# Strided sparse attention feeding a squared-ReLU MLP on one Trainium2 core: moving DMA transposes two groups later and one pair of steps past each other

## The chip, the core and the metric

The kernel runs on one core of a Trainium2 chip. A core has five engines with their own instruction streams: TensorE (PE; its weight loads are listed as PEld), VectorE (DVE), ScalarE (ACT), GpSimd (POOL) and SyncE (SP). SP only issues DMA transfers here; POOL issues some too. The metric is the device time of one execution in microseconds (us). Before the change the median of four runs is 313.06 us.

## What is computed

Inputs are q, k, v of shape (8, 8, 576, 64) and two weights, w_in (512 x 2048) and w_out (2048 x 512), in fp32.

```
scores = q k^T / 8
heads 0-3: keep  0 <= row - col < 32              (local)
heads 4-7: keep  row >= col and row = col mod 32  (strided)
attn   = softmax(scores) v            for every batch and head
x      = attn, heads side by side     4608 x 512
out    = relu(x w_in)^2 w_out         4608 x 512
```

## The kernel before, in words

**Units.** The attention is cut into 32 units, u = 4 b + p: batch b, pair of heads p. Pairs 0 and 1 are local, 2 and 3 strided. A local head has six blocks of 96 rows; a strided head has eight groups of 72 rows (rows are brought together by their number mod 8, and a mask picks the right ones).

**Steps of a unit.** They are small closures in a list:

- `step_T(u, "q")`, `step_T(u, "k")`: PE transposes q or k into PSUM (L271), ACT or DVE copies the result to SBUF (L284, L286). Only early units have them (`has_T`: local units of batches 0 to 3, strided ones of batches 0 and 1). For later ones DMA transposes do this work: `transpose_str` (L161, both strided pairs of a batch at once, from a bf16 copy in DRAM that POOL's casting DMA has written, L153) and `transpose_local` (L173).
- `step_S(u)`: scores on PE (L315) into four PSUM banks, the exponential on ACT (L320), and, on DVE, the mask (L326).
- `step_D(u, part)`: the PV step. PE multiplies the exponentials with v and a column of ones (L419), DVE takes the reciprocal of the sums (L433) and multiplies (L434) into `x_l` (local) or `x_s` (strided). Local units have two parts, strided ones three.
- `step_E(u)`: brings the result, transposed, into `xt[p]`, the left operand of the MLP. Local units of batches 2 to 7 do it with one DMA transpose on SP's queue (L444). Others use PE transposes (L451) and a copy (L457 to L459).
- `step_X(u)`: for strided units of batches 6 and 7, a store to DRAM and a DMA transpose back (L471, L473), the second of them six groups later.

**The MLP.** It runs in 9 chunks of 512 rows. `mm1(c, ff)` is a group of four matmuls of 512 columns (L487) over the four pairs in the order 0, 1, 2, 3, and then a ReLU on ACT (L493) and a square on DVE (L494). `mm2(c, i)` is a group of four matmuls with w_out (L527); each fourth one ends a block of 128 rows, which ACT copies to `y` (L531) and SP stores (L532). Rows of batch b are 576 b to 576 b + 575, so chunk 2 needs batches 1 and 2, chunk 3 batches 2 and 3, chunk 4 batches 3 and 4, chunk 5 batches 4 and 5.

**What sets the order.** Everything is written out by hand at build time. Units of batch 0 go first (`first_steps`). Then a list of groups (mm1 and mm2) is walked through; ahead of each group come as many attention steps as a due table says, and the hooks of that place (loads of later batches). The list of steps is made by `stream_steps`, once for batch 1 and once for the rest. `later(n, fn)` puts something off by n groups: `tick`, after each group, runs what is due.

Each engine works through its own stream in order, and a waiting instruction holds up all behind it. For the change the following matter:

- On PE, in batch 1: S(5), T(6, q), D(4, 0), T(6, k), D(4, 1), S(6), with groups of mm2 between them. D(4, 0) needs v of unit 4, which POOL's casting DMA loads (L214) and whose last 32 rows of each block POOL then shifts (L221). The same POOL stream has issued, ahead of that, the four transfers of v for the strided units 6 and 7 (L227).
- PSUM tiles of the attention come from a pool of five banks that go round in the order of the program (`ps_t`).
- On SP: loads of q, k, v (L107, L113, L185, L201), the DMA transposes and the stores of y, all in one queue. Each of the eight semaphores that tell of landings is used in turn, so a transfer isn't issued before the one eight places ahead of it has landed.

Of the kernel before, what the change touches and what calls it, by code (L numbers as in the profile page):

```python
# [14 lines left out]
def kernel(  # L15
# [9 lines left out]
    nc = tc.nc  # L25
# [69 lines left out]
    def is_local(u):  # L95
        return units[u][1] < H // 4
# [146 lines left out]
    def later(n, fn, key=None):  # L243
        pending.append((clock[0] + n, key, fn))
# [12 lines left out]
    def step_T(u, name):  # L257
        s = st[u]
        local = is_local(u)
        n, w = (6, QL) if local else (NJ, SP_)  # L260
        src = s[name]
        if u != 1:
            src = src.rearrange("p j h d -> p (j h d)" if local else "p h c -> p (h c)")
        pt = ps_t.tile([128, S], BF16, name="pt")
        for j in range(n):
            if u == 1:
                for h in range(2):
                    nc.tensor.transpose(pt[64 * h:64 * h + 64, w * j:w * (j + 1)],
                                        src[:, h, D * j:D * (j + 1)], ident[0:w, 0:w])
            else:  # L270
                nc.tensor.transpose(pt[:, w * j:w * (j + 1)], src[:, 128 * j:128 * (j + 1)],  # L271
                                    ident[0:w, 0:w])
        if local and name == "k":
            full = kTl[v_slot(u)]
            dst = full[:, 32:32 + S]
        else:
            full = dst = qkT.tile([128, S], BF16, name=f"{name}T")
        if local:
            o = dst.rearrange("c (p j) -> c p j", j=6)
            i = pt.rearrange("c (j p) -> c p j", j=6)  # L280
        else:
            o, i = dst, pt
        if name == "q" and u not in (1, 2, 3):
            nc.scalar.copy(o, i)  # L284
        else:
            nc.vector.tensor_copy(o, i)  # L286
        s[name + "T"] = full
# [149 lines left out]
    def step_E(u):  # L437
        s = st[u]
        b, p = units[u]
        x = s["x"]  # L440
        local = is_local(u)
        n, w = (NL, QL) if local else (NJ, SP_)
        if local and b >= XB:
            nc.sync.dma_start_transpose(  # L444
                out=xt[p][:, b * S:(b + 1) * S].rearrange("c (t q) -> c t q", q=QL),
                in_=x.rearrange("p n d -> p (n d)"))
            st.pop(u)
            return
        px = ps_t.tile([128, S], BF16, name="pt")
        for t in range(n):  # L450
            nc.tensor.transpose(px[:, w * t:w * (t + 1)],  # L451
                                x[:, 2 * t:2 * t + 2, :].rearrange("p h d -> p (h d)"),
                                ident[0:w, 0:w])
        dst = xt[p][:, b * S:(b + 1) * S]
        copy = nc.scalar.copy if u < 12 else nc.vector.tensor_copy
        if local:
            copy(dst, px)  # L457
        else:
            copy(dst.rearrange("c (p j) -> c p j", j=NJ),  # L459
                                  px.rearrange("c (j p) -> c p j", j=NJ))  # L460
        st.pop(u)
# [3 lines left out]
    def by_dram(u):  # L465
        return not is_local(u) and units[u][0] >= XD

    def step_X(u):
        b, p = units[u]
        t = dram.tile([S, 2 * D], BF16, name="x_d")  # L470
        nc.sync.dma_start(out=t.rearrange("(p j) c -> p (j c)", j=NJ),  # L471
                          in_=st.pop(u)["x"].rearrange("p n d -> p (n d)"))
        later(6, lambda: nc.sync.dma_start_transpose(out=xt[p][:, b * S:(b + 1) * S], in_=t))  # L473
# [60 lines left out]
    T_ = lambda u, nm: (lambda: step_T(u, nm))  # L534
    S_ = lambda u: (lambda: step_S(u))
    D_ = lambda u, part: (lambda: step_D(u, part))
    E_ = lambda u: (lambda: step_E(u))

    idle_w = y_pool.tile([128, 512], FP32, name="y").bitcast(BF16)
# [49 lines left out]
    def has_T(u):  # L589
        return units[u][0] < (LB if is_local(u) else XB)  # L590

    def stream_steps(lo, hi, order, ends, last=None):
        add_ = order.append

        def finish(u):
            if not by_dram(u):
                add_(E_(u))
                ends[u] = len(order)

        if last is None:  # L600
            add_(T_(lo, "q"))
        else:
            finish(last)
        for i in (T_(lo, "k"), T_(lo + 1, "q"), S_(lo), T_(lo + 1, "k"), lambda: None):
            add_(i)
        for u in range(lo, hi):
            if u + 1 < hi:
                add_(S_(u + 1))
            if u + 2 < hi and has_T(u + 2):
                add_(T_(u + 2, "q"))  # L610
            if u > lo and is_local(u):
                finish(u - 1)
            add_(D_(u, 0))
            if u > lo and not is_local(u):
                finish(u - 1)
            if u + 2 < hi and has_T(u + 2):
                add_(T_(u + 2, "k"))
            add_(D_(u, 1))
            if not is_local(u):
                add_(D_(u, 2))  # L620
            if by_dram(u):
                add_(lambda u=u: step_X(u))
                ends[u] = len(order)
        if hi < 4 * B:
            add_(T_(hi, "q"))
        else:
            finish(hi - 1)
# [96 lines left out]
    NCH = T // 512  # L724
    steps, ends = [], {}
    stream_steps(4, 8, steps, ends)
    stream_steps(8, 4 * B, steps, ends, last=7)
    groups = []
    starts = {}
# [113 lines left out]
```

## Time and profile before

| | us |
|---|---|
| median of 4 runs | 313.06 |
| the runs | 312.82, 313.30, 314.43, 311.17 |
| the profiled execution, its own time | 312.82 |
| its span, first to last instruction | 310.9 |
| PE busy | 300.0 (96%) |
| PE weight loads | 148.4 (48%) |
| DVE busy | 166.7 (54%) |
| ACT busy | 162.8 (52%) |
| POOL busy | 90.1 (29%) |
| SP's DMA queue | 72528 packets, 32.98 MB |
| POOL's DMA queue | 19552 packets, 10.98 MB |

All durations below come from the one profiled execution; 1.9 us of its time lie outside of its span. A row of a timeline gives the start, the length, the engine (SPq is SP's queue), the line of the code, the operation, its output and inputs, shapes, a count where instructions were merged, and in brackets idle time of the engine ahead of it with what ended it. Matmuls overlap, so lengths of neighbouring rows on PE add up to more than the time between them. For a transfer the row shows its issue; when it landed is told by the completion records of the trace.

### The profile page before, as it was taken

How to read it: one execution, taken by the hardware profiler on the slowest of the kernel's cores; microseconds unless marked ns; L12 is line 12 of the kernel's file. 1: busy time of each engine (PE TensorE's matmuls, PEld its weight loads, DVE VectorE, ACT ScalarE, POOL GpSimd, SP SyncE). 2: the span in 40 equal slices, each digit the busy share in tenths (PEclk: the TensorE clock that was granted, in tenths of full speed). 3: DMA queues.
4: the chain of work that ended last, by engine and by line, in shares of the span. 5: the costliest groups of instructions: out<-in, count | busy, mean ns of one | idle time of the engine just before them, and what ended most of it. 6: DMA issues, size and time to landing. Idle time of an engine off the chain costs nothing.

```text
span 310.9 us, 6192 instructions
## 1 busy us (share of the span) xinstructions
PE 300.0 (96%) x2368; PEld 148.4 (48%) x2368; DVE 166.7 (54%) x411; ACT 162.8 (52%) x338; POOL 90.1 (29%) x117
## 2 busy tenths in 40 slices
PE   7889897999999999999999999999999999999995
PEld 3534454544555544454444454444444444444444
DVE  7675666379766886576467676654422222222200
ACT  3957654387654765555555555655443434344311
POOL 8528864554720723381066033000000000000000
PEclk9999999799999999999999999999999999999999
DMA  7999999999999999999999792224122010000021
GB/s 143 155 206 215 210 191 259 215 260 195 198 136 230 206 211 162 201 246 209 158 225 205 167 207 78 73 72 55 53 76 84 34 37 34 34 34 36 39 96 67
DMA packets 92252, 44.40 MB, mean 143 GB/s; under 512 B 76544, under 2 KB 85536, under 8 KB 92032
## 3 DMA queue, kind: packets, MB, share of 16 engines
q1 hardware_dynamic: 72528, 32.98, 49.2%
q0 software_dynamic: 19552, 10.98, 25.9%
q8 instruction: 18, 0.29, 0.4%
q14 instruction: 10, 0.08, 0.1%
q10 hardware_dynamic: 144, 0.07, 0.1%
HBM read 36.70 MB, written 13.57 MB: 162 GB/s over the span
## 4 chain that ended last, share of the span: by engine, by line
PE 87%; DMA 7%; ACT 2%; POOL 2%; DVE 1%; issue 1%; DVEq 0%; ACTq 0%; POOLq 0%
PE ph L487 40%; PE py L527 27%; PE ph L527 9%; DMA vs<-in_v_dram 5%; PE pt L419 4%; PE pt L315 3%; DMA qT_s<-in_q_dram 2%; PE pt L271 1%; PE pt L451 1%; POOL vs L227 1%; ACT e L320 1%; PE pt L512 1%; PE ph L512 1%; ACT g_sb L371 0%; ACT g_sb L370 0%
## 5 line engine op out<-in xcount | busy, mean ns | idle before, releaser
L487 PE MATMUL ph<-xt,w_in_b 128*128 128x512 bf16 x572 | 143.5, 379 | 0.3 <-ACT r L493 0.3
L493 ACT ACTIVATE r<-ph 128x512 bf16<-128x512 f32 x143 | 85.4, 598 | 94.0 <-PE ph L487 92.6
L494 DVE TENSOR_TENSOR g_sb<-r 128x512 bf16<-128x512 bf16 x144 | 71.8, 502 | 103.3 <-ACT r L493 102.7
L527 PE MATMUL py<-w_out_b,g_sb 128*128 128x512 bf16 x400 | 102.7, 379 | 0.0
L487 PEld LDWEIGHTS <-w_in_b 128*128 128x128 bf16 x576 | 52.4, 98 | 56.6 <-issue 0.5
L527 PEld LDWEIGHTS <-g_sb 128*128 128x128 bf16 x560 | 51.1, 98 | 54.0 <-issue 0.8
L320 ACT ACTIVATE e<-pt 128x288 bf16<-128x288 f32 (+1 forms) x128 | 46.4, 408 | 14.3 <-PE pt L315 14.3
L527 PE MATMUL ph<-w_out_b,g_sb 128*128 128x512 bf16 x160 | 40.8, 390 | 0.0
L419 PEld LDWEIGHTS <-e 128*128 128x128 bf16 (+1 forms) x392 | 20.9, 98 | 17.1 <-issue 1.7
L434 DVE TENSOR_TENSOR x_s<-pt,rinv 72x384 bf16<-72x384 f32 (+1 forms) x42 | 21.4, 509 | 1.5
L192 POOL CAST vl<-vl_st 128x768 bf16<-128x768 f32 x8 | 7.6, 950 | 48.7 <-DMA vl_st<-in_v_dram 39.4
L326 DVE TENSOR_TENSOR e<-e,mask_loc 128x576 bf16<-128x576 bf16 x32 | 16.9, 529 | 3.1 <-ACT e L320 3.1
L326 DVE TENSOR_TENSOR e<-e,mask_str 72x576 bf16<-72x576 bf16 x32 | 16.1, 508 | 3.3 <-ACT e L320 3.2
L123 POOL CAST k_l<-k_st 96x768 bf16<-96x768 f32 x14 | 12.8, 913 | 17.5 <-DMA k_st<-in_k_dram 17.5
L531 ACT COPY y<-py 128x512 f32<-128x512 f32 x25 | 14.7, 587 | 5.4 <-PE py L527 5.2
L433 DVE RECIPROCAL rinv<-pt 96x6 f32<-96x6 f32 (+2 forms) x70 | 12.8, 183 | 6.5 <-PE pt L419 6.2
L434 DVE TENSOR_TENSOR x_l<-pt,rinv 96x384 bf16<-96x384 f32 x28 | 15.5, 553 | 1.0
L123 POOL CAST q_l<-q_st 96x768 bf16<-96x768 f32 x14 | 12.7, 909 | 10.5 <-DMA q_st<-in_q_dram 7.5
L419 PE MATMUL pt<-vs,e 72*128 72x65 bf16 x224 | 13.7, 196 | 1.9 <-DMA vs<-in_v_dram 1.9
L531 ACT COPY y<-ph 128x512 f32<-128x512 f32 x10 | 5.9, 590 | 15.8 <-PE ph L527 15.8
L208 POOL CAST vs<-v_st 72x1024 bf16<-72x1024 f32 x12 | 13.3, 1136 | 0.4
L545 PE MATMUL py<-y 128*128 128x512 bf16 x24 | 8.7, 450 | 1.3 <-DVE y L687 1.3
(91 smaller groups left out, 166.9 us busy)
## 6 DMA issues: line engine op xcount, KB each, us to landing
out_dram<-y SPq DMA_DIRECT2D x35, 256.0 KB, 2.8
v_st<-in_v_dram SPq DMA_DIRECT2D x12, 288.0 KB
q_st<-in_q_dram SPq DMA_DIRECT2D x16, 144.0 KB, 5.2
k_st<-in_k_dram SPq DMA_DIRECT2D x16, 144.0 KB, 7.1
vl_st<-in_v_dram SPq DMA_DIRECT2D x16, 144.0 KB, 3.1
w_in_b<-in_moe_w_in_dram POOLq DMA_DIRECT2D x4, 512.0 KB, 12.2
w_out_b<-in_moe_w_out_dram POOLq DMA_DIRECT2D x4, 512.0 KB, 10.5
q_st<-in_q_dram SPq DMA_DIRECT2D x7, 288.0 KB, 6.9
```

What stands on the lines that cost most here:

```text
L123: copy(t.rearrange("p j h d -> p h j d"), s[name + "f"].rearrange("p h (j d) -> p h j d", j=6))
L208: (copy or nc.gpsimd.tensor_copy)(t[:, :, 0:D], s["vf"].rearrange("p h (j d) -> p (h j) d", d=D))
L320: nc.scalar.activation(e[0:kn, lo:lo + S // 2], banks[row][half][0:kn, 0:S // 2], AF.Exp, scale=scale)
L326: nc.vector.tensor_tensor(x, x, m.to_broadcast([kn, n, w]), op=ALU.mult)
L419: nc.tensor.matmul(po[:, n - n0, :], e[0:kn, pos(n):pos(n) + 128], rhs[0:kn, src(n), 0:D + 1], start=True, stop=True)
L433: nc.vector.reciprocal(rinv[0:w, 0:m], po[0:w, 0:m, D:D + 1])
L434: nc.vector.tensor_tensor(x, po[0:w, 0:m, 0:D], rinv[0:w, 0:m].to_broadcast([w, m, D]), op=ALU.mult)
L487: nc.tensor.matmul(ph, w_in_b[:, kk, 128 * ff:128 * (ff + 1)], xt[kk][:, 512 * c:512 * (c + 1)], start=(kk == order[0]), stop=(kk == order ...
L493: nc.scalar.activation(r, ph, AF.Relu)
L494: later(1, lambda: nc.vector.tensor_tensor(g[:, ff, :], r, r, op=ALU.mult))
L527: nc.tensor.matmul(py, g[:, ff, 128 * j:128 * (j + 1)], w_out_b[:, ff, :], start=(ff == 0), stop=(ff == 15))
L531: nc.scalar.copy(y, py)
```

## The change

Two edits. The DMA transpose in `step_E` is handed to `later` with two groups instead of being issued at once. And in `stream_steps`, at unit 4 alone, the transposes of the next strided k (unit 6) are put ahead of the first PV step of unit 4.

```diff
         if local and b >= XB:
-            nc.sync.dma_start_transpose(
+            later(2, lambda: nc.sync.dma_start_transpose(
                 out=xt[p][:, b * S:(b + 1) * S].rearrange("c (t q) -> c t q", q=QL),
-                in_=x.rearrange("p n d -> p (n d)"))
+                in_=x.rearrange("p n d -> p (n d)")))
             st.pop(u)
             return
...
             if u > lo and is_local(u):
                 finish(u - 1)
+            ahead = u + 2 < hi and has_T(u + 2)
+            if ahead and u == 4:
+                add_(T_(u + 2, "k"))
+                ahead = False
             add_(D_(u, 0))
             if u > lo and not is_local(u):
                 finish(u - 1)
-            if u + 2 < hi and has_T(u + 2):
+            if ahead:
                 add_(T_(u + 2, "k"))
             add_(D_(u, 1))
```

In the compiled streams nothing is added or taken away on any engine. On PE one block of 8 transposes and one of 6 PV matmuls change places, with their followers on DVE. On SP the 12 transposes of L444 stay in the queue, most of them one to three places further back:

```
SP, before                      SP, after
xt unit 8                       xt unit 8
xt unit 9                       qT_s, kT_s of batch 4
qT_s, kT_s of batch 4           store y
store y x2                      xt unit 9
...                             store y
store y                         ...
xt unit 12                      store y
qT, kTl of unit 17              qT, kTl of unit 17
xt unit 13                      xt unit 12
store y                         store y
                                xt unit 13
```

## The prediction

> **What bounds the kernel now.** I read the page's row of busy tenths first, then the table by stage, then the list of what TensorE waited for, and last the timeline round each place that the change touches.
>
> Page, part 2 (40 slices of 7.8 us):
>
> ```profile
> PE   7889897999999999999999999999999999999995
> PEclk9999999799999999999999999999999999999999
> DMA  7999999999999999999999792224122010000021
> ```
>
> TensorE is full from slice 8 on, and the clock dips once, in slice 8. The stage table says where it isn't full. Columns: stretch, length, busy time of PE, PEld, DVE, ACT, POOL with instruction counts, granted clock, DMA share, GB/s.
>
> ```profile
> 36.00:40.00 4.00, 3.01 (x39) 1.64 (x40) 2.85 (x6) 1.87 (x6) 3.63 (x5) 1.00 1.73 187
> 40.00:46.00 6.00, 6.00 (x78) 3.52 (x77) 3.92 (x9) 3.77 (x11) 4.20 (x7) 1.00 1.48 187
> 46.00:52.00 6.00, 6.00 (x79) 3.51 (x78) 4.19 (x11) 3.69 (x9) 1.71 (x2) 1.00 1.27 251
> 52.00:55.00 3.00, 1.14 (x17) 0.58 (x16) 0.84 (x4) 0.20 (x1) 1.65 (x2) 1.00 1.33 251
> 55.00:59.00 4.00, 4.00 (x31) 2.02 (x28) 1.96 (x6) 0.64 (x1) 0.88 (x2) 0.57 1.49 165
> 59.00:97.00 38.00, 37.93 (x403) 20.18 (x400) 27.62 (x66) 25.36 (x59) 18.71 (x22) 1.00 1.19 213
> 97.00:233.00 136.00, 136.00 (x1075) 66.61 (x1074) 85.16 (x206) 75.21 (x157) 36.29 (x42) 1.00 0.77 154
> 233.00:294.00 61.00, 61.00 (x284) 27.66 (x283) 15.34 (x36) 25.93 (x45) 0.00 (x0) 1.00 0.11 42
> ```
>
> From 59 to 294 us TensorE lacks 0.07 us of busy time, and starts of consecutive 512-column matmuls lie 216 ns apart both at 97 to 233 and at 233 to 294, where nothing else runs. So there is nothing to win after 59. The one loss that lies beside the change is at 52 to 59:
>
> ```profile
> 53.71 0.19 PE L419 MATMUL pt<-vs,e 72*128 72x65 bf16 x1 [1.15 <-DMA vs<-in_v_dram]
> 54.61 0.31 PE L419 MATMUL pt<-vs,e 72*128 72x65 bf16 x5 [0.71 <-DMA vs<-in_v_dram]
> ```
>
> These are the first PV matmuls of unit 7, which stand still until the two halves of its v land. The trace's completion records (sixteen for a transfer) put the landings at 53.58 and 54.57. The clock is then granted at 0.57 over 55 to 59: 4 x (1 - 0.57) = 1.7 us of work lost. Stall and clock together are 1.15 + 0.71 + 1.7 = 3.6 us. The chain of waits agrees: its piece before that matmul is the DMA of vs, 15.06 us from 39.51.
>
> **Part two of the change, T(6,k) ahead of D(4,0).** Nothing is added or removed: 8 transposes and one DVE copy change places with 6 PV matmuls, a reciprocal and a multiply.
>
> ```profile
> 40.73 0.42 PE L271 MATMUL pt<-ident,qT_s 72*128 72x72 bf16 x8
> 40.99 0.44 PE L419 MATMUL pt<-vl,e 128*128 128x65 bf16 x6
> 41.27 1.03 PE L527 MATMUL ph<-w_out_b,g_sb 128*128 128x512 bf16 x4
> 42.13 0.42 PE L271 MATMUL pt<-ident,kT_s 72*128 72x72 bf16 x8
> 42.39 0.35 PE L419 MATMUL pt<-vl,e 128*128 128x65 bf16 x6
> ```
>
> - What it can save. D(4,0) waits for GpSimd's shift of unit 4's v (L221). Its first matmul starts at 40.989, its second at 41.120, against 0.03 us between the others: a wait of 0.10 us. With the 8 transposes (0.26 us from start to start) and one group of four matmuls (0.86) in front of it, D(4,0) would start near 42.1, 1 us after the shift ended. Saved: 0.10 us.
> - What it could cost. kT_s of unit 6 landed at 34.83, so the transposes needn't wait. Their PSUM bank is the first of S(5)'s, whose exponential was over near 40.2. On DVE the copy of kT comes early (near 41.5 to 41.9), then the mask of 0.46, then both pairs of reciprocal and multiply (0.18 + 0.55 each), ending near 43.9 against 43.74 now. S(6), which starts at 43.53 and takes four banks, now waits in its last bank for D(4,0)'s multiply, near 43.2: in time. Unit 4's transposes (45.07) need the multiply that ends at 43.9. Cost 0; 0.2 us if the DVE order slips.
> - What becomes of either. All of this lies ahead of 53.71, where TensorE stands waiting for a landing. Those v transfers were issued by GpSimd at 38.52 and 39.51, before the moved step, and nothing of the moved step is queued ahead of them. TensorE arriving 0.1 us earlier waits 0.1 us longer; arriving up to 1.15 + 0.71 us later costs nothing. **Worth: 0.0 us**, bounds -0.1 and +0.2.
>
> **Part one, the transposes of local x two groups later.** It is 12 DMA transposes on SP's queue. By the compiled order of SP: unit 8's keeps its place; unit 9's goes behind the two big strided transposes of batch 4 and one y store; unit 12's behind the two local transposes of unit 17; units 13, 16, 17, 20 and 21 each behind one y store; units 24, 25, 28 and 29 keep theirs. They read x_l, finished long before (unit 9's multiply ends at 77.67), so no DVE wait is removed from the queue. SP is simply late: it issues without a break over this stretch.
>
> ```profile
> 83.94 5.97 SPq L444 DMA_TRANSPOSE xt<-x_l  x2
> 90.02 1.29 SPq L161 DMA_TRANSPOSE qT_s<-q_d  x1
> 91.41 2.08 SPq L161 DMA_TRANSPOSE kT_s<-k_d  x1
> 93.58 1.00 SPq L532 DMA_DIRECT2D out_dram<-y  x2
> ```
>
> - What it can save. y stores and strided transposes go out 1 to 4 us earlier. Nobody waits for them: no ACT wait for a y buffer and no TensorE wait for these transposes stands in the list of waits. 0.0 us.
> - What it can cost. Each transpose must land before the first matmul of the chunk that reads it. Landings now, from the completion records: unit 9 at 93.47, unit 13 at 109.35, unit 17 at 142.97, unit 21 at 168.89. The first groups of chunks 2, 3, 4 and 5 start at 97.11, near 113.0, at 145.01 and near 176.9, and need those units with their second matmul, 0.22 us later. So the spare time is 3.9, 3.9, 2.3 and 8.2 us.
> - How much of it goes. Landings on SP's queue follow the order of issue here, so putting a transfer behind others gives it, nearly, the landing of the last one it passed: the same bytes go through. Unit 9 takes the place of the y store that landed at 96.54; unit 13 that of 110.08; unit 17 that of 143.62; unit 21 that of 171.28. Spare then: 97.33 - 96.54 = **0.8 us**, 3.1, 1.6 and 5.9 us. No wait appears. **Worth: 0.0 us.**
>
> Bounds for unit 9: its issue now stands behind kT_s of batch 4, which can't be issued before k_d has landed (89.93). 1.3 us for that issue, 0.53 for the store and 2.4 from issue to landing (the page's median for these transposes) give 94.2 at the earliest; the next store in the queue, 97.69, is the latest. The late end is a stall of 0.4 us. I take 96.5, nearest to the row that it swaps with. If the cover is gone, TensorE stops at the head of chunk 2, with every later matmul behind it: microsecond for microsecond.
>
> Two rules of the Trainium skill bear on this. "DMA: Bandwidth & Descriptors", section on queues, rings and completion order, says that completion isn't in issue order for one issuing engine; by it the swap could land a transfer earlier or later, about 1.1 us here (the spacing 93.47, 94.53, 95.64, 96.54), so unit 9 at 97.6 and a stall of 0.3. The rows of this stretch land in order, so I keep 0. The other prices a stall: "TensorE: Matmul & The Clock Gate", section "What's actually happening", lets the clock drop to half after an idle window of about 3.4 us. By it a stall of 2 us costs 2. The row above is harsher: 1.9 us of idle, split in two, brought 1.7 us of half clock. I price by the row: 2 us of stall costs near 3.7.
>
> **Sum.** The profiled execution took 312.82 with a span of 310.9, so 1.9 lies around the span. 310.9 + 0.0 + 0.0 + 1.9 = 312.8, which is 0.24 under the median of the four runs (313.06, from 311.17 to 314.43). Carried to the median: **313.1**.
>
> **Rivals.**
> - *Slower: unit 9's transpose becomes the last input of chunk 2.* It is one mechanism, k_d's landing. Now unit 9 doesn't depend on it; afterwards it stands behind it in the queue. In the profile k_d took 7.1 us (82.86 to 89.93); of the six k_d transfers one took 13.9. The spare 0.8 us is gone when k_d lands 0.8 us later. It is worth over 1% once the stall is near 1.9 us, k_d 2.7 us later, 3.6 with the clock: 316.7. Against it: five of the six took 6.1 to 7.2, and the DMA engines had idle time at 92 to 93. A stall of 0.3 to 1.4 us without a clock drop, 313.4 to 314.5, is its mild form.
> - *Faster: the stall of unit 7 and its clock drop go.* 3.6 us less: 309.5. For it: it is the only loss in the middle. Against it: it is ended by transfers issued before the moved step. It decides only if v lands 1.9 us earlier.
> - *The change does nothing that can be seen* is my forecast itself: the moves happen, and all of them lie under cover.
>
> **How the numbers follow.** No change 0.70; the mild stall 0.14; the slow case 0.10; the fast case 0.06. A difference of 1% (3.1 us) is about what a measurement of this kernel tells from none. So faster 0.06, within 1% 0.84, slower 0.10. The range: the four runs reach 1.9 below and 1.4 above their median, of which a median of runs moves perhaps half; below I add what is left of the fast case, above the mild stall and the start of the slow one: 311.0 to 315.6.
>
> **What would show it.** Right: D(4,0) starts near 42.1 without the 0.10; the wait for vs is longer by about as much or unchanged; unit 9's landing is near 96.5 and TensorE has no gap at 97; 59 to 294 stays full. Wrong: a gap before the first L487 of chunk 2 put down to an xt transfer, perhaps with a clock under 1.00 after it; or a landing of vs well before 53, with the dip at 55 gone.

## The result, and the profile after

| | before | after |
|---|---|---|
| median, us | 312.92 (64 runs) | 314.11 (43 runs) |
| lowest, us | 310.65 | 311.12 |
| ratio to before, 95% interval | | 1.003 [1.0011, 1.0049] |
| profiled execution, its span, us | 312.82, 310.9 | 315.57, 313.6 |

The ratio, here and below, leaves out executions more than 1.5% above the fastest of their kernel (the profiled one of e1_later_only is such a one); the medians leave out none. 0.3% of 312 us is 0.9 us, with an interval of 0.3 to 1.5: slower, but within the 1% that the forecast called no change. The median lies 1.0 us over the 313.1 that was forecast and inside its range, 311.0 to 315.6.

The page's costliest group in the profile after has a new releaser in its last column:

```profile
L487 PE MATMUL ph<-xt,w_in_b 128*128 128x512 bf16 x572 | 144.4, 380 | 1.8 <-DMA xt<-x_l 1.4
```

Before, the idle time ahead of L487 was 0.3 us, all of it put down to ACT. Now 1.4 more stands against a transfer that writes xt. The table by stage (length, busy of PE, PEld, DVE, ACT, POOL, clock, DMA share, GB/s) says where:

```profile
36.00:40.00 4.00, 3.82 (x41) 1.78 (x39) 3.25 (x6) 2.46 (x6) 4.00 (x5) 1.00 1.79 183
40.00:46.00 6.00, 5.92 (x87) 3.63 (x88) 3.94 (x10) 3.35 (x10) 5.45 (x9) 1.00 1.32 199
46.00:52.00 6.00, 5.87 (x75) 3.35 (x73) 3.58 (x11) 3.70 (x9) 0.90 (x2) 1.00 1.42 210
52.00:55.00 3.00, 1.62 (x12) 0.64 (x10) 1.28 (x4) 0.90 (x2) 1.74 (x2) 1.00 1.31 283
55.00:59.00 4.00, 3.56 (x30) 1.91 (x30) 1.58 (x6) 0.64 (x1) 1.65 (x2) 0.61 1.55 210
59.00:97.00 38.00, 37.81 (x401) 20.05 (x400) 26.95 (x64) 25.25 (x59) 18.50 (x22) 1.00 1.21 206
97.00:233.00 136.00, 134.50 (x1071) 65.97 (x1068) 85.89 (x207) 73.75 (x155) 35.05 (x42) 1.00 0.80 157
233.00:294.00 61.00, 61.00 (x285) 27.64 (x283) 14.91 (x35) 26.27 (x45) 0.00 (x0) 1.00 0.11 42
```

Up to 59 us it is the old picture: a stall at 52 to 55 and a clock of 0.61 after it. New is the row of 97 to 233, which lacks 1.5 us and lacked nothing before. The timeline of PE shows the places:

```profile
42.57 0.76 PE L419 MATMUL pt<-vl,e 128*128 128x65 bf16 x12
...
55.44 0.31 PE L419 MATMUL pt<-vs,e 72*128 72x65 bf16 x5 [1.81 <-DMA vs<-in_v_dram]
...
146.18 0.38 PE L487 MATMUL ph<-xt,w_in_b 128*128 128x512 bf16 x1
148.00 0.81 PE L487 MATMUL ph<-xt,w_in_b 128*128 128x512 bf16 x3 [1.44 <-DMA xt<-x_l]
```

First row: D(4,0) and D(4,1), the two PV steps of unit 4, now run as one block. Second: the stall at unit 7 has stayed. Last two: the first matmul of chunk 4, for pair 0, starts at 146.18; the second, for pair 1, must wait for unit 17. It starts 1.82 us later instead of 0.22: 1.60 lost. Before, the matmuls at the heads of chunks 2 and 4 ran without a gap (eight and four, merged):

```profile
97.11 1.89 PE L487 MATMUL ph<-xt,w_in_b 128*128 128x512 bf16 x8
...
145.01 1.03 PE L487 MATMUL ph<-xt,w_in_b 128*128 128x512 bf16 x4
```

At the head of chunk 2 the same distance is 0.44 (starts at 98.06 and 98.50), so 0.22 lost there. That makes 1.8 of the 2.7 us by which this profile is longer. The other 0.9 were there when chunk 2 began (98.06 against 97.11), after a spell of half clock from 18.3 to 21.7 that lies ahead of everything the change touches.

### The profile page after: what moved, and what is told of

The parts are those of the page before. It is cut to its first block, busy times and chain, and to the rows that moved or that the text cites. A ratio compares the mean times of both kernels' runs of the same rounds, so it can differ in the third digit from the quotient of the medians.

```text
span 313.6 us, 6193 instructions
## 1 busy us (share of the span) xinstructions
PE 301.9 (96%) x2368; PEld 149.1 (48%) x2368; DVE 165.5 (53%) x411; ACT 162.9 (52%) x338; POOL 88.7 (28%) x117
## 4 chain that ended last, share of the span: by engine, by line
PE 74%; DMA 16%; POOL 4%; DVE 3%; issue 1%; ACT 0%; DVEq 0%; POOLq 0%; ACTq 0%
PE ph L487 34%; PE py L527 25%; PE ph L527 7%; DMA vs<-in_v_dram 5%; DMA w_in_b<-in_moe_w_in_dram 5%; DMA vl<-in_v_dram 4%; DMA xt<-x_l 3%; PE pt L419 3%; PE pt L315 3%; DVE e L326 1%; DVE g_sb L494 1%; PE pt L451 1%; POOL kT_s L133 1%; POOL qT_s L133 1%; PE pt L512 1%
## 5 line engine op out<-in xcount | busy, mean ns | idle before, releaser
L487 PE MATMUL ph<-xt,w_in_b 128*128 128x512 bf16 x572 | 144.4, 380 | 1.8 <-DMA xt<-x_l 1.4
L494 DVE TENSOR_TENSOR g_sb<-r 128x512 bf16<-128x512 bf16 x144 | 70.9, 495 | 105.8 <-ACT r L493 105.4
L487 PEld LDWEIGHTS <-w_in_b 128*128 128x128 bf16 x576 | 52.4, 98 | 58.7 <-issue 2.9
L192 POOL CAST vl<-vl_st 128x768 bf16<-128x768 f32 x8 | 6.7, 841 | 44.9 <-PE ph L487 18.1
```

Source lines behind the costliest of these rows:

```text
L487: nc.tensor.matmul(ph, w_in_b[:, kk, 128 * ff:128 * (ff + 1)], xt[kk][:, 512 * c:512 * (c + 1)], start=(kk == order[0]), stop=(kk == order ...
L494: later(1, lambda: nc.vector.tensor_tensor(g[:, ff, :], r, r, op=ALU.mult))
```

## The experiments

Three theories were set against each other. In the measured ratios below the time of the kernel before is 1. A: units 9 and 17 land too late for chunks 2 and 4. B: the swap of the steps costs the time. C: the change itself costs nothing, and only the first 60 us of the executions differ.

**Only the transposes later.**

```diff
-            if ahead and u == 4:
+            if ahead and u == -1:
```

> Only the transposes go two groups later; the steps T(6,k) and D(4,0) stay as before. Theory A (spare time on SP's queue: units 9 and 17 land too late for chunks 2 and 4 in part of the executions): the whole loss is here, ratio to before 1.003, and the profile shows gaps of 0 to 2 us at the head of chunk 2 or 4 put down to an xt transfer. Rival B (the swap of the steps costs the time): 1.000 and no such gap. Rival C (the executions differ only in how the first 60 us go, whatever the change): 1.000, with gaps as often as before.

Measured: 312.54 (22 runs), ratio 1.0009 [0.9983, 1.0036]. The interval holds both 1.000 and 1.003, so the times decide nothing. The timeline of PE does:

```profile
39.85 0.20 PE L419 MATMUL pt<-vl,e 128*128 128x65 bf16 x1
41.45 0.31 PE L419 MATMUL pt<-vl,e 128*128 128x65 bf16 x5 [1.40 <-POOL vl L221]
...
55.76 0.31 PE L419 MATMUL pt<-vs,e 72*128 72x65 bf16 x5 [2.84 <-DMA vs<-in_v_dram]
...
98.03 0.38 PE L487 MATMUL ph<-xt,w_in_b 128*128 128x512 bf16 x1
99.11 0.81 PE L487 MATMUL ph<-xt,w_in_b 128*128 128x512 bf16 x3 [0.69 <-DMA xt<-x_l]
```

The last two rows are theory A's gap at chunk 2: 1.08 from start to start, so 0.86 lost, with unit 9 landing at 99.06. The first two rows show what the swap is good for: without it TensorE stood 1.40 us for GpSimd's shift of v at unit 4.

**Only the swap.** The reverse: the diff's second edit alone, with the transpose issued at once as before.

```diff
-            later(2, lambda: nc.sync.dma_start_transpose(
+            nc.sync.dma_start_transpose(
```

> Only T(6,k) goes ahead of D(4,0); the transposes are issued at once as before. Theory A: 1.000, since TensorE waits for the v of unit 7 afterwards in any case. Rival B: 1.003. Rival C: 1.000.

Measured: 313.45 (22 runs), ratio 1.0006 [0.9975, 1.0038]. No gap at chunks 2 or 4. Theory B has nothing in its favour: no stall stands at unit 4 or at S(6), the stall for v has moved on to unit 6 (2.05 at 49.69), and this kernel's profile is the shortest of the first six (span 310.0). By the time alone a loss of 0.3% by the swap isn't excluded.

**The change without units 9 and 17.** `put` issues the transpose.

```diff
-            later(2, put)
+            later(2, put) if u not in (9, 17) else put()
```

> The change as it is, but the transposes of units 9 and 17 are issued at once, so these two keep their places in SP's queue. Theory A: 1.000, unit 17 lands before chunk 4 begins by about 2 us, unit 9 before chunk 2 by about 4. Rival B: 1.003 (the swap is in it). Rival C: 1.000.

Measured: 312.9 (22 runs), ratio 1.0013 [0.9988, 1.0039]. No gap for xt. Unit 9 landed 2.1 us ahead of its need, unit 17 only 0.5: less than expected.

**Earlier than before.** In the kernel before, the transpose is issued at the end of the second PV step.

```diff
+        if is_local(u) and b >= XB and part == 1:
+            nc.sync.dma_start_transpose(
...
```

> The kernel before, with each local DMA transpose of x issued right behind its second PV step, so ahead of the eight loads (unit 17) or behind fewer transfers (unit 8). Theory A: unit 17 lands near 135 to 138 instead of 143, so chunk 4 can't wait for it; if the kernel before loses time there in some executions this gains up to 0.3% (0.997 to 1.000). Rivals B and C: 1.000. If SP stops for x_l and holds up loads: up to 1.003.

Measured: 312.59 (22 runs), ratio 1.0009 [0.9984, 1.0034]. Unit 17 landed at 132.82, 11.9 us ahead of chunk 4. No gain can be told from none, so nothing shows that the kernel before was losing time there.

**Unit 17 alone, and much later.**

```diff
-            later(2, put)
+            later(12, put) if u == 17 else put()
```

> The changed kernel, but of the transposes of x only unit 17's is put off, by 12 groups, so that it stands behind both strided transposes of batch 6, two y stores and two local transposes; all others are issued at once. Theory A (what counts is the landing of unit 17 against the second matmul of chunk 4): it lands where the second of those local transposes landed, 148.7 in the profile before and 154.1 in the profile after, against a need at 145.2 and 146.4: TensorE stands for 3.5 to 8 us at the head of chunk 4, and, if 1.9 us of idle cost a clock drop as at unit 7, 1.7 us more: ratio 1.011 to 1.031. Rivals B and C (the place of these transposes doesn't matter at all): 1.000.

Measured: 318.72 (4 runs), ratio 1.0173 [1.0106, 1.0241], with this at the head of chunk 4:

```profile
144.94 0.38 PE L489 MATMUL ph<-xt,w_in_b 128*128 128x512 bf16 x1
148.34 0.81 PE L489 MATMUL ph<-xt,w_in_b 128*128 128x512 bf16 x3 [3.02 <-DMA xt<-x_l]
```

(This kernel has two lines more, so L489 is L487.) The landing at 148.30 ends the wait: 3.40 from start to start, 3.18 lost in this execution, a little under the range. The interval is 3.3 to 7.5 us. The place of a single transfer of 96 x 768 values in SP's queue moves the kernel by over 1%. Theories B and C, which gave 1.000 for this kernel, missed. It shows the mechanism at twelve groups, not at two. The profiled execution is the fastest of the four (315.89), so what the others lost beyond its 3.18 us isn't explained by this trace.

**Mixed: early, but batch 3 later.** `put_x` issues the transpose; the first hunk is in `step_E`, the second at the end of `step_D`.

```diff
+            if b == 3:
+                later(2, lambda: put_x(u, x))
...
+        if is_local(u) and XB <= units[u][0] != 3 and part == 1:
+            put_x(u, s["x"])
```

> Steps as before. The local transposes of x are issued right behind their second PV step, except in batch 3, where they go two groups later, behind the two local transposes of unit 17. Theory A: no gap for xt at the heads of chunks 2 to 5 and none for kTl near 109 (0.55 to 0.76 us in three of the profiles so far): 0.997 to 1.000 of before, 0.995 to 0.998 of the changed kernel. Rival C: 1.000.

Measured: 312.71 (22 runs), ratio 0.999 [0.9961, 1.0019]. No gap for xt or kTl in its profile, and no gain that can be told from none.

**Holding back unit 7.** `hold[0]` is the place of D(7, 0) in the list of steps.

```diff
+    for g in range(28, 31):
+        due[g] = min(due[g], hold[0])
```

> The kernel before, with the first PV step of unit 7 and all steps behind it held back by two groups of mm2. It measures what the stall at unit 7 and its clock drop are worth, which the forecast put at 3.6 us. If that holds: TensorE arrives 1.7 us later at the landing of v, the stall falls to 0.2 to 0.7, the clock doesn't drop, 2 to 3 us are won (0.990 to 0.994), less up to 1 us for the end of unit 7 now coming right before chunk 1. If the clock drops anyway or the steps crowd together: 0.998 to 1.003.

Measured: 312.22 (22 runs), ratio 1.0001 [0.9976, 1.0026]. The stall at unit 7 was gone, and the clock stayed at 1.00 (same columns as in the table by stage):

```profile
53.00:56.00 3.00, 3.00 (x40) 1.80 (x37) 0.89 (x4) 0.53 (x1) 1.10 (x2) 1.00 1.34 281
56.00:59.00 3.00, 2.26 (x21) 1.30 (x22) 1.47 (x5) 1.94 (x4) 1.65 (x2) 1.00 1.62 179
```

Chunk 2 began at 95.18 instead of 97.11, though this execution had lost 1.7 us to half clock at 19 to 22. Then its timeline of PE gives the gain back:

```profile
99.56 0.43 PE L315 MATMUL pt<-qT,kTl 64*128 64x96 bf16 x12 [0.64 <-DMA kTl<-k_l]
...
109.88 0.43 PE L315 MATMUL pt<-kT,kTl 64*128 64x96 bf16 x12 [1.25 <-DMA kTl<-k_l]
```

0.64 + 1.25 = 1.9 us of waiting for the transposed k of units 16 and 17, which come through the same SP queue.

**The change once more.** One execution, for a second trace.

> The changed kernel once more, one look. Theory A: unit 9 lands within 1 us of the start of chunk 2 and unit 17 within 2 us of that of chunk 4, on either side, with a gap wherever it is late; the kernel before had 2.3 us and more. Rival B: a stall near unit 4's first PV step or at S(6). Rival C: no gap for xt, a different first 60 us.

Measured: 313.35. The head of chunk 2:

```profile
97.12 0.38 PE L487 MATMUL ph<-xt,w_in_b 128*128 128x512 bf16 x1
97.66 1.02 PE L487 MATMUL ph<-xt,w_in_b 128*128 128x512 bf16 x4 [0.16 <-DMA xt<-x_l]
```

0.54 from start to start, so 0.32 lost; at chunk 4 the distance is 0.43, 0.22 lost. Both transfers were late again.

**Two attempts at a better version.** The first joins the swap, the hold at unit 7 and the mixed order; the second also has ACT issue the stores of y.

> The swap at unit 4, unit 7 held back by two groups, and the transposes of x as in the mixed version (early, but two groups later in batch 3). Theory F (behind 60 us SP's queue sets a floor of its own; what TensorE wins at unit 7 is given back at the local k of unit 17, near 109): the mixed order takes one transfer away from ahead of that k, so some of the 3 us is kept: 0.993 to 0.998. Rival G (the DMA engines' bytes, not the order of the queue, set the floor): 1.000.

Measured: 311.55 (14 runs) beside 311.48 for the kernel before on that chip, ratio 0.9996 [0.9962, 1.003]. The expected gain didn't come. No wait for xt or kTl stands in its profile. But TensorE came to unit 7 early, in spite of the hold (52.56), and v no earlier (54.51), so a stall of 1.79 stayed.

```diff
             nc.scalar.copy(y, py)
-            nc.sync.dma_start(out=out[r0:r0 + 128, :], in_=y)
+            nc.scalar.dma_start(out=out[r0:r0 + 128, :], in_=y)
```

> The combined version, with the stores of y issued by ACT instead of SP. Of SP's queue some eight stores of 0.5 us each go between 60 and 150 us. Theory F: the transposes of x and k land up to 4 us earlier, no gap for xt or kTl: 0.988 to 0.995. Rival G: the same bytes through the same engines, 0.997 to 1.000. If ACT is held up by its issues: above 1.000.

Measured: 318.83 (6 runs), ratio 1.0242 [1.019, 1.0293]. Expected was a gain. The profile (span 319.7, clock 0.978; at 321.67 us longer than most of the six) has half clock at 53 to 60 and at 91 to 94. In it the first store went out at 49.90, 10 us earlier than in e9_combined (59.95), while v of unit 6 was under way; its second half landed at 54.52 instead of 47.14, and TensorE stood for v for 1.23 and 3.49 us. But its first half, at 46.82 in e9_combined, hadn't landed when that store went out either, so the store is not the whole cause, and the cause stays open. No version here beats the kernel before by a difference that can be measured.

## Why the forecast was right, point by point

**No gain from the swap: right, for the reason given, though its size was off.** The forecast let D(4,0) save 0.10 us, from the one profile. In the other executions without the swap the same wait was 1.40 (e1_later_only), 1.25 (e4_early), 1.20 (e6_mixed_early) and 0.09 us (e7_hold_unit7); in those with it (the two of the changed kernel, e2_swap_only, e3_not_9_17, e5_unit17_late) it is at most 0.24. So the edit does what it is for, in the executions in which that wait is long. It brings nothing, because TensorE then stands for v of unit 6 or 7 until it lands: 2.84, 2.35 and 1.97 us of stall followed in the three executions that had lost time at unit 4; where the swap had saved that, 1.81 followed in the profile after, 2.05 (at unit 6) in e2_swap_only, 2.21 in e5_unit17_late, 2.62 in three pieces in e3_not_9_17, 3.57 (at unit 6) in e8_changed_again. The ratio of the swap alone, 1.0006, bears it out to within 0.4%.

**The transposes land about 3 us later: right.** The forecast gave unit 9 the landing of the last transfer that it passes, 3.07 us later. To take out how far each execution had got, count from the landing of k_d of batch 4. Unit 9 landed 3.5, 3.0 and 3.5 us after it in before, e2_swap_only and e7_hold_unit7, and 6.7, 6.8 and 6.8 after it in the changed kernel, e1_later_only and e8_changed_again: 3.4 us later. Landings kept the order of issue in this stretch, as assumed. The Trainium skill's statement that completion isn't in issue order ("DMA: Bandwidth & Descriptors", section "Queues, rings and completion order") made no difference here. One figure was misread: the 2.4 us from issue to landing rests on a single late transfer (186.58 to 188.95), while unit 9 itself took 7.5 before the change and 3.0 to 3.2 after it. It entered the earliest bound only.

**No wait appears: wrong, by the term "spare time".** The forecast took it from one execution: 3.9 us for unit 9, 2.3 for unit 17. What the profiles show, as landing ahead of the need (negative: late):

| profile | unit 9 | unit 17 |
|---|---|---|
| before | 3.9 | 2.3 |
| e2_swap_only | 2.5 | 1.1 |
| e7_hold_unit7 | 1.6 | 1.8 |
| e3_not_9_17 | 2.1 | 0.5 |
| e5_unit17_late | 5.4 | (moved by 12 groups) |
| after | -0.2 | -1.6 |
| e1_later_only | -0.8 | 0.7 |
| e8_changed_again | -0.3 | -0.2 |

The upper five rows have the transfers in their old place (unit 17 in four of them), the lower three two groups later. With 1.6 to 5.4 us to spare for unit 9 and 0.5 to 2.3 for unit 17, a delay of 3.4 mostly shows: all three profiles of the lower rows have a gap for xt, none of the others has one with the transfer in its old place. Theory C, by which gaps are as frequent as before, doesn't fit that. TensorE lost 1.82, 0.86 and 0.54 us at the two heads in the lower three, 1.1 in the mean, beside 0.9 [0.3, 1.5] in the measured times. The forecast's number held because this loss is small, not because its zero was right: a stall of 3 us would have carried the median out of its range. The loss is the forecast's mild rival (chance 0.14), with one part that it had not seen: it looked to unit 9 alone, since unit 17's spare time was put at 1.6 after the move, while most of the loss in the profile after, 1.60 of 1.82, is unit 17's.

**A second, smaller step that failed: "the same bytes go through".** The forecast gave a moved transfer the landing of the one it passed, and the rest of the queue no delay. In the old order unit 9's issue falls into a stretch in which SP's queue is held up anyway: in before none of its transfers landed from 85.07 to 90.24, while q_d and k_d were under way, and the issue took 3.99 us, against 1.23 in the profile after. e2_swap_only has the old order:

```profile
84.02 5.80 SPq L444 DMA_TRANSPOSE xt<-x_l  x2
89.93 2.08 SPq L161 DMA_TRANSPOSE qT_s<-q_d  x1
92.10 1.27 SPq L161 DMA_TRANSPOSE kT_s<-k_d  x1
93.47 1.11 SPq L532 DMA_DIRECT2D out_dram<-y  x2
94.67 1.24 SPq L173 DMA_TRANSPOSE qT<-q_l  x1
```

and the changed kernel:

```profile
85.85 2.30 SPq L444 DMA_TRANSPOSE xt<-x_l  x1
90.08 1.93 SPq L161 DMA_TRANSPOSE qT_s<-q_d  x1
92.10 2.39 SPq L161 DMA_TRANSPOSE kT_s<-k_d  x1
94.58 0.53 SPq L532 DMA_DIRECT2D out_dram<-y  x1
95.21 1.23 SPq L444 DMA_TRANSPOSE xt<-x_l  x1
96.53 0.63 SPq L532 DMA_DIRECT2D out_dram<-y  x1
97.26 1.24 SPq L173 DMA_TRANSPOSE qT<-q_l  x1
```

From 88.15 to 90.08 SP now stands still: q_d landed at 90.03. (In e8_changed_again q_d landed at 88.17; SP stood still for 0.7 us only, but the issue of qT_s then took 3.05.) The moved issue of 1.23 us comes behind it. Counted from the landing of k_d again, the transpose in the last row starts 4.7, 4.5 and 5.0 us later in before, e2_swap_only and e7_hold_unit7, and 5.5, 5.8 and 5.8 in the three with the new order: the rest of the queue is late by 1.0 us more. e3_not_9_17 isolates the cause: it is the changed kernel with units 9 and 17 in their old places, and there the figure is 4.7. Counted in the same way, unit 17 landed after 53.0, 53.2 and 53.2 us in the old order, and after 56.2, 54.0 and 54.9 in the new: 1.9 later in the mean, where the forecast allowed 0.65 (142.97 to 143.62).

**The slow and the fast rival.** A stall large enough for 1% didn't come at two groups; e5_unit17_late, at twelve, shows the mechanism at 1.7%. The fast one was overpriced. Taking the stall at unit 7 away (e7_hold_unit7) gave 1.0001, not 3.6 us, since the k of units 16 and 17 then ended the next waits, 1.9 us of them in its trace. "Nothing to win after 59" hid that between 97 and 147 TensorE and SP's queue run within 0.5 to 5.4 us of each other, by the table of spare times.

What stays open: the times of the single parts can't be told apart, as their intervals are 0.5% wide. That the loss belongs to units 9 and 17 rests on the gaps in three traces and on e5_unit17_late, not on the ratios of e1_later_only and e3_not_9_17. Neither is it known why SP's queue and TensorE keep so different a distance from one execution to the next.

## What to carry to other kernels

A transfer's spare time from a single trace is a sample: before a transfer is put later, compare it in several traces, and ask whether the delay is smaller than the least of them. When a wait is removed, look for the next absolute time that TensorE must meet, here a landing, since up to there the gain is only moved. And in a queue issued in order, an entry that fills a wait costs nothing where it is: moved behind the wait, it holds up all that follow (here by 1.0 us, for an issue of 1.23).

## What the runs showed of the hardware

The clock drop after a stall is not set by the length of the stall alone. In before 1.86 us of idle (in two pieces) brought half clock for 3.4 us; in the profile after, 1.81 us did. In e5_unit17_late 3.02 us of idle brought none, and in e4_early 2.35 us brought none:

```profile
41.21 0.31 PE L419 MATMUL pt<-vl,e 128*128 128x65 bf16 x5 [1.25 <-POOL vl L221]
...
55.02 0.31 PE L419 MATMUL pt<-vs,e 72*128 72x65 bf16 x5 [2.35 <-DMA vs<-in_v_dram]
```

```profile
53.00:56.00 3.00, 0.98 (x16) 0.70 (x16) 0.59 (x2) 0.37 (x1) 1.03 (x2) 1.00 1.28 230
56.00:59.00 3.00, 3.00 (x35) 1.75 (x33) 1.41 (x5) 1.29 (x3) 0.82 (x1) 1.00 1.76 148
```

The clock (third number from the right) is 1.00 in both rows, though TensorE had worked for 0.98 of the first 3 us. The clock records of each trace change only at whole multiples of 3.41 us from one another (after 13.65, 3.41, 34.13 and 3.41 us in the profile after). Cut into stretches of 3.41 us that begin at such a change, the traces show the idle time of before (1.86) and of the profile after (1.81) each inside one stretch, with half clock in the next; the 2.35 us of e4_early are cut by a border at 54.19 into 1.52 and 0.83. The Trainium skill, page "TensorE: Matmul & The Clock Gate", section "What's actually happening", says that the window of observation runs freely, which fits. It also gives an idle window of about 3.4 us as what brings half clock; here 1.81 us did, and the measurement decides. But the place of a stall isn't all: 1.87 of the 3.02 us in e5_unit17_late, and all 1.79 us in e9_combined, lie in one stretch too, and brought no drop. So neither the forecast's price (1.7 us at 1.9 of idle) nor a whole idle window gives the cost of one stall, and what does stays open.
